# Moving the start-up loads of an attention-and-FFN kernel into one casting queue, with single-head transposes and masks by matmul

## The chip, the cores and the metric

The kernel runs on one core of a Trainium2 chip. The metric is device time in microseconds (us), the median over several executions; lower is better. A ratio between two kernels is the mean time of the one's fast runs over the mean of the other's fast runs of the same rounds, so it is not quite the ratio of the medians that stand beside it. An interval in brackets is a 95% interval. "Same" means within 2%.

Engine names in the profile: PE is TensorE's matmuls, PEld its weight loads, DVE VectorE, ACT ScalarE, POOL GpSimd, SP SyncE. A group or timeline line names the source line (L323), the engine, the operation, the tiles as output<-input, and the shapes.

## The reference, cut to what matters

```python
# q, k, v: (batch 4, heads 8, seq 768, dim 64); mem_k, mem_v: (4, 8, 8, 64)
chunk, left_ctx, right_ctx = (32, 16, 8)
for c in range(seq // chunk):                    # each chunk of 32 queries sees its 56 or fewer
    q_c   = q[:, :, c*32 : c*32+32]              # neighbouring keys and 8 memory keys
    k_full = concat([mem_k, k[:, :, l_start:r_end]], axis=2)
    v_full = concat([mem_v, v[:, :, l_start:r_end]], axis=2)
    a = exp(scale * q_c @ k_full.T - max);  a = a / (sum(a) + 1e-9)
    out[:, :, c*32 : c*32+32] = a @ v_full
x = out.transpose(0, 2, 1, 3).reshape(3072, 512)
result = (maximum(x @ w_gate, 0) * (x @ w_val)) @ w_out     # d_ff = 1536
```

## The kernel before: the parts that matter here

The 3072 tokens are eight blocks of 384. Each block has an attention part (scores, exponentials, values) and an FFN part: 12 gate/value units of eight matmuls each (4 for `g_ps`, 4 for `vl_ps`), then three output units. While the FFN of one block keeps TensorE busy, the attention of the next is slipped in. Only the first two blocks (the "start blocks") have nothing to hide behind: their k, q and v come in as f32 by plain DMA, ACT and POOL cast them, TensorE transposes a pair of heads at a time, and DVE and ACT copy the result out of PSUM.

```python
class StartBlock(Block):                                   # blocks 0 and 1
    def cast_k(self, h):
        self.by_pair(nc.scalar.copy, self.kc, self.kr, h)  # ACT: f32 -> bf16, pairs of heads
    ...
    def keys_turn(self, h):
        ps = self.k_ps = fps.tile([128, 2, KR, KW], BF16, tag="gv", name="k_ps")
        for i in range(2):
            for s in range(KR):
                nc.tensor.transpose(ps[:, i, s, 0:KP], self.kc[:, 2 * h + i, s], ids["b"][:KP, :KP])
    # keys_copy: DVE copies k_ps to kb;  queries_copy: ACT and DVE copy q_ps to qz

class LaterBlock(Block):                                   # blocks 2 to 7
    ...
    def cast_k(self):
        ...
        pin(nc.vector.tensor_copy(self.kn[:, :, 0:3], view[:, :, 0:3]))
        nc.vector.tensor_copy(self.kn[0:24, :, 3], view[0:24, :, 3])      # NOT pinned
```

`pin` keeps an instruction in program order. An instruction without it may be placed elsewhere on its engine when the program is built. The last line above: the small cast of block 2.

```python
def warm(n, cols=256): ...                 # matmuls on zeros, to keep TensorE's clock up
warm(12, 512)
...
start_attention(b0, attention(b0, order0),
                lambda i: warm((5, 0, 4, 8, 2, 2, 2, 2, 2)[i]), first_weights)
...                                        # weights by POOL's queue, b1's k, q, v by SP's
def second_loads():
    for f in b2.pieces(sp):                # block 2's loads are issued first,
        f()
    pool_after(2, b2.qf[0:KROWS, 0, 0:1])
    for c in range(0, NDC, 4):             # then w_out, in three pieces
        pool(w_out_sb[:, c:c + 4], ...)
```

The softmax here doesn't subtract the row's maximum and nothing guards it: scores larger than these inputs give would overflow.

Of the kernel before, what the change touches and what calls it, by code (L numbers as in the profile page):

```python
# [17 lines left out]
def kernel(  # L18
# [33 lines left out]
    KW = KP + 2  # L52
    MEMCOL = 400
# [25 lines left out]
    ex_t = [wpool.tile([128, 4, 128], F16, name=f"ex{i}") for i in range(4)]  # L79
# [71 lines left out]
    def build_sel(T):  # L151
        base, starts = block_starts(T, KR * KROWS)
        sel = wpool.tile([KP, KR, NJ, 128], F16, name=f"sel{T}")
        (nc.vector if T == 0 else nc.gpsimd).memset(sel.bitcast(F32), 0.0)
        odd, first = regular(T)
        rel = [s - base for s in starts]
        for sl, r0, steps in ((sel[:, :, first:first + 3], rel[first], [[QB, 3]]),
                              (sel[:, :, odd], rel[odd], [])):
            nc.gpsimd.affine_select(
                out=sl, in_=sl, pattern=[[-1, KR]] + steps + [[1, 128]], compare_op=ALU.not_equal,  # L160
                fill=1.0, base=r0 - NMEM, channel_multiplier=-KR)
        nc.gpsimd.memset(sel[:, :, :, 0:NMEM], 0.0)
        sl = sel[:, :, :, 0:NMEM]
        nc.gpsimd.affine_select(
            out=sl, in_=sl, pattern=[[-1, KR], [0, NJ], [1, NMEM]], compare_op=ALU.not_equal,
            fill=1.0, base=KR * KROWS, channel_multiplier=-KR)
        return sel
# [3 lines left out]
    def kind_of(qb):  # L171
        return "first" if qb == 0 else ("last" if qb == NQB - 1 else "int")

    class Block:


        def __init__(self, n):
# [5 lines left out]
            self.qf = vpool.tile([128, H, NT * D], F32, name="qf")  # L183
# [12 lines left out]
        def load_q(self, h0, nh, dma):  # L196
            dma(self.qf[:, h0:h0 + nh], self.rows(q, h0, nh, MB * self.T, 128, NT * D))

    class StartBlock(Block):


        def make(self):
            self.kr = kf_t[self.n][0:KP].rearrange("p t h d -> p (t h d)").rearrange("p (h r) -> p h r", h=H)
            self.vr = vf_t[self.n][0:KP].rearrange("p t h d -> p (t h d)").rearrange("p (h r) -> p h r", h=H)
            self.kc, self.qc = kn_t[self.n][0:KP], qn_t[self.n]
            self.vc = spool.tile([KP, H, KR * D], F16, name="vc")

        def load_kv(self, which, h0, nh, dma):
            t, dst = (k, self.kr) if which == "k" else (v, self.vr)
            dma(dst[0:KROWS, h0:h0 + nh], self.rows(t, h0, nh, self.kbase, KROWS, KR * D))  # L210

        def load_mem(self, dma):
            for m, dst in ((mem_k, self.kr), (mem_v, self.vr)):
                dma(dst[KROWS:KP], self.mem(m, 0, H, KR * D))

        def cast_k(self, h):
            self.by_pair(nc.scalar.copy, self.kc, self.kr, h)

        def cast_q(self, h):
            self.by_pair(nc.scalar.copy, self.qc, self.qf, h)  # L220

        def by_pair(self, op, dst, src, h):
            op(dst[:, 2 * h:2 * h + 2].rearrange("p a s (x d) -> p a s x d", x=2),
               src[:, 4 * h:4 * h + 4].rearrange("p (a x) (s d) -> p a s x d", x=2, d=D))

        def cast_v(self, h):
            pin(nc.gpsimd.tensor_copy(self.vc[:, 4 * h:4 * h + 4], self.vr[:, 4 * h:4 * h + 4]))

        def keys(self, h):
            self.keys_turn(h)  # L230
            self.keys_copy(h, 0)
            self.keys_copy(h, 1)

        def keys_turn(self, h):
            ps = self.k_ps = fps.tile([128, 2, KR, KW], BF16, tag="gv", name="k_ps")
            for i in range(2):
                for s in range(KR):
                    nc.tensor.transpose(ps[:, i, s, 0:KP], self.kc[:, 2 * h + i, s], ids["b"][:KP, :KP])

        def keys_copy(self, h, part):  # L240
            ps = self.k_ps

            def band(row, mids, n):
# [3 lines left out]
            rel = [(s - self.kbase) // KR for s in self.starts]  # L247
            odd, first = regular(self.T)
            m = NMEM // KR
            nc.vector.tensor_copy(  # L250
                kb[:, part, first:first + 3, m:],
                bass.AP(tensor=ps.tensor, offset=ps.offset + KR * KW * part + rel[first],
                        ap=[ps.ap[0], [QB // KR, 3], [1, BAND // KR], [KW, KR]]))
            if part == 0:
                return
            nc.vector.tensor_copy(kb[:, :, odd, m:], band(rel[odd], [], BAND // KR))
            nc.vector.tensor_copy(kb[:, :, :, 0:m], band(KROWS, [[0, NJ]], m))  # L257
# [5 lines left out]
        def queries_turn(self, h):  # L263
            ps = self.q_ps = fps.tile([128, 2, NT, 128], BF16, tag="gv", name="q_ps")
            for i in range(2):
                for s in range(NT):
                    nc.tensor.transpose(ps[:, i, s], self.qc[:, 2 * h + i, s], ids["b"])
# [16 lines left out]
    class LaterBlock(Block):  # L284


        def make(self):
            self.kf, self.vf = kf_t[self.n % 2], vf_t[self.n % 2]
            self.kn, self.qn = kn_t[self.n % 2], qn_t[self.n % 2]
            self.qT = spool.tile([128, HP, NT, 128], BF16, name="qT")  # L290
            self.kT = spool.tile([128, HP, 512], BF16, name="kT")

        def pieces(self, dma):
# [18 lines left out]
            return [k01, k12, lambda: self.load_q(0, H, dma)] + [v1(j) for j in range(NJ)]  # L312
# [44 lines left out]
    def quad_stages(blk, j, g, x_big):  # L357
        st = {}
        kind, on_pe = kind_of(NJ * blk.T + j), blk.n == 0
# [99 lines left out]
    def load_start(blk):  # L459
        for h0 in (0, 4):  # L460
            blk.load_kv("k", h0, 4, sp)
            blk.load_q(h0, 4, sp)
            blk.load_kv("v", h0, 4, sp)

# [4 lines left out]
    gate = wpool.tile([128, 4], F32, name="gate")  # L469
    here = wpool.tile([1, 4], F16, name="here")  # L470

    def pool_after(i, src):
        pin(nc.gpsimd.tensor_copy(gate[0:KROWS, i:i + 1], src))
# [4 lines left out]
    b0.load_mem(nc.scalar.dma_start)  # L478
    load_start(b0)
    ids["b"] = wpool.tile([128, 128], BF16, name="ident_b")  # L480
    make_identity(nc, ids["b"])
    ids["h"] = wpool.tile([128, 128], F16, name="ident_h")
    nc.vector.tensor_copy(ids["h"], ids["b"])


    nc.vector.memset(w_out_sb[:, 0, :], 0.0)  # L486

    def warm(n, cols=256):
        ps = fps.tile([128, 512], F32, tag="gv", name="warm_ps")
        for _ in range(n):  # L490
            pin(nc.tensor.matmul(ps[:, 0:cols], lhsT=w_out_sb[:, 0, 0:128], rhs=w_out_sb[:, 0, 0:cols],  # L491
                                 start=True, stop=True))

    warm(12, 512)
    ids["chunks"] = build_chunks()
    lows["first"] = build_low("low_first", NMEM - 16)
    lows["int"] = build_low("low_int", NMEM)
    sels[0] = build_sel(0)
    for t in qz_t[0:1]:
        nc.vector.memset(t[0:D, :, 1].bitcast(F32), 0.0)  # L500
        nc.vector.memset(t[D:128, :, 0].bitcast(F32), 0.0)
    for t in vb_t:
        nc.vector.memset(t[:, :, :, D:VW], 1.0)
    for t in ex_t:
        nc.vector.memset(t[:, :, QB:128], 0.0)

    order0 = [(j, g) for g in range(2) for j in range(NJ)]

    def in_text_order(first):

        last = {}
        for ins in nc.cur_bb.bb.instructions[first:]:
            if ins.engine in (mybir.EngineType.PE, mybir.EngineType.DVE, mybir.EngineType.Activation):
# [5 lines left out]
    def start_attention(blk, att, fill, at_k1=lambda: None):  # L519

        scores, out_of, turn = ([a[i] for a in att] for i in range(3))
        blk.cast_k(0)
        blk.keys(0)
        blk.cast_q(0)
        blk.queries_turn(0)
        fill(0)
        blk.queries_copy(0)
        blk.cast_v(0)
        scores[0]()
        scores[1]()  # L530
        blk.values(0, 0)
        scores[2]()
        at_k1()
        fill(1)
        blk.cast_k(1)
        blk.values(2, 0)
        scores[3]()
        out_of[0]()
        out_of[1]()
        blk.keys(1)  # L540
        fill(2)
        blk.cast_q(1)
        blk.queries_turn(1)
        out_of[2]()
        blk.queries_copy(1)
        out_of[3]()
        blk.cast_v(1)
        fill(3)
        scores[4]()
        scores[5]()  # L550
        blk.values(0, 1)
        scores[6]()
        blk.values(2, 1)
        scores[7]()
        out_of[4]()
        fill(4)
        out_of[5]()
        turn[4]()
        fill(5)
        out_of[6]()  # L560
        turn[5]()
        fill(6)
        out_of[7]()
        turn[6]()
        fill(7)
        turn[7]()
        fill(8)

    def first_weights():
        pool_after(0, b0.kr[0:KROWS, 4, 0:1])  # L570
        weights(0, 512)

    first = len(nc.cur_bb.bb.instructions)
    start_attention(b0, attention(b0, order0), lambda i: warm((5, 0, 4, 8, 2, 2, 2, 2, 2)[i]), first_weights)
    in_text_order(first)

    weights(512, 1024)
    weights(1024, 1536)
    sp_after(0, w_gate_sb[0:1, 0, 1024:1025])
    b1.load_mem(sp)  # L580
    load_start(b1)
    sels[1] = build_sel(1)
    for t in qz_t[1:]:
        nc.gpsimd.memset(t[0:D, :, 1].bitcast(F32), 0.0)
        nc.gpsimd.memset(t[D:128, :, 0].bitcast(F32), 0.0)
    for name, qb in (("first", 0), ("int", 1), ("last", NQB - 1)):
        masks[name] = build_mask("mask_" + name, qb)

    order = [(j, g) for j in range(NJ) for g in range(2)]
# [29 lines left out]
    first = len(nc.cur_bb.bb.instructions)  # L619
    for u in range(8):  # L620
        dff[0][u]()

    def second_loads():
# [64 lines left out]
```

## Time and profile before

| | before |
|---|---|
| device time, median of the first 3 runs | 254.0 us (252.83 to 254.27) |
| span of the profiled run | 251.2 us |
| TensorE busy | 233.0 us, 93% |
| block 0's first gate matmul | 25.37 us |
| block 1's first gate matmul | 57.20 us |

The page's first two parts, for the kernel before. In the slices each digit is the busy share in tenths of 1/40 of the span (6.3 us here); PEclk is the clock granted to TensorE in the same tenths.

```profile
PE 233.0 (93%) x1647; PEld 139.4 (55%) x1647; DVE 137.2 (55%) x358; ACT 116.7 (46%) x221; POOL 58.3 (23%) x116
PE   7689987779979998999999999999999999999993
PEclk9799999997999999999999999999999999999999
```

TensorE is nearly full from slice 13 on (nines, with one 8). Whatever a change of the start can bring lies in the first twelve digits.

The timeline of TensorE, kernel before. Columns: start in us, length in us, engine, line, operation, tiles, shapes, count; in brackets the idle time just before and what ended it.

```profile
7.75 0.57 PE L238 MATMUL k_ps<-ident_b,kn_103 114*128 114x114 bf16 x8 [1.55 <-ACT kn_103 L223]
25.37 0.81 PE L427 MATMUL g_ps<-xT,w_gate_sb 128*128 128x384 f16 x4 [0.34 <-ACT xT L401]
36.79 0.57 PE L238 MATMUL k_ps<-ident_b,kn_104 114*128 114x114 bf16 x8 [0.86 <-ACT kn_104 L223]
57.20 1.44 PE L427 MATMUL g_ps<-xT,w_gate_sb 128*128 128x384 f16 x4 [0.57 <-ACT xT L401]
```

Four marks: block 0's keys are turned at 7.75 us, its FFN starts at 25.37, block 1's keys are turned at 36.79 and its FFN starts at 57.20. From the last mark to the end of the span it takes 251.2 - 57.2 = 194.0 us, nearly all of it TensorE's own work. The first group of that FFN took 1.44 us for four matmuls where 0.81 is usual.

Two windows of the kernel before. Columns after the window and its length: busy us and instruction count of PE, PEld, DVE, ACT and POOL, then the granted clock, the DMA engines' busy share and GB/s.

```profile
36.00:46.00 10.00, 7.74 (x77) 5.79 (x78) 6.57 (x14) 6.54 (x12) 3.36 (x5) 1.00 1.10 207
46.00:58.00 12.00, 8.15 (x84) 5.41 (x83) 9.66 (x29) 6.62 (x13) 8.99 (x16) 0.95 1.19 227
```

And the small cast of block 2 on DVE, from the timeline of the kernel before:

```profile
44.71 0.85 DVE L319 CAST kn_103<-kf_99 24x512 bf16<-24x512 f32 x1 [0.56 <-DMA kf_99<-in_k_dram]
```

Being free, it was placed in the middle of block 1's attention. It waited for its data by 0.56 us there.

### The profile page before, as it was taken

The page shows a single profiled execution, that of the slowest core. Times are in us where ns is not written, and L with a number is a line of the kernel's source. Part 1 is how long each engine was busy: PE and PEld are TensorE (multiplying, and loading weights), DVE is VectorE, ACT ScalarE, POOL GpSimd, SP SyncE. Part 2 cuts the span into 40 slices and gives each one's busy share as a digit, 9 for nine tenths or more (in the row PEclk, how much of TensorE's full clock was granted, in tenths as well). Part 3 has the DMA queues.
Part 4 walks back from the last instruction along what each step waited for, and adds up shares of the span by engine and source line. Part 5 has one row for each costly group of instructions (what it writes and reads, how often), then busy time and mean ns, then how long its engine had stood idle before and what let it go on. Part 6 is the DMA issues. An engine that isn't in the chain of part 4 may idle for free.

```text
span 251.2 us, 4576 instructions
## 1 busy us (share of the span) xinstructions
PE 233.0 (93%) x1647; PEld 139.4 (55%) x1647; DVE 137.2 (55%) x358; ACT 116.7 (46%) x221; POOL 58.3 (23%) x116
## 2 busy tenths in 40 slices
PE   7689987779979998999999999999999999999993
PEld 2477545454546445664566456645665566556541
DVE  5375336882577306995289527952796178404410
ACT  1666355653544245672467146714672366223311
POOL 8789002682001203034004012340022000000000
PEclk9799999997999999999999999999999999999999
DMA  6999999998798678998599949994999401130012
GB/s 185 235 176 207 163 274 202 243 203 138 149 251 156 157 175 215 253 130 186 171 266 133 195 142 260 169 147 155 263 161 171 143 0 33 37 119 7 3 42 84
DMA packets 95873, 40.17 MB, mean 160 GB/s; under 512 B 76330, under 2 KB 92778, under 8 KB 95850
## 3 DMA queue, kind: packets, MB, share of 16 engines
q1 hardware_dynamic: 91062, 35.12, 66.5%
q0 software_dynamic: 4752, 4.72, 11.7%
q8 instruction: 13, 0.21, 0.4%
q14 instruction: 10, 0.08, 0.1%
q10 hardware_dynamic: 36, 0.03, 0.1%
HBM read 30.43 MB, written 6.29 MB: 146 GB/s over the span
## 4 chain that ended last, share of the span: by engine, by line
PE 72%; DMA 17%; DVE 4%; POOL 2%; issue 2%; SPq 1%; ACT 1%; DVEq 0%; POOLq 0%
PE out_ps L446 24%; PE vl_ps L431 21%; PE g_ps L427 21%; DMA kf_99<-in_k_dram 7%; DMA w_gate_sb<-in_moe_w_gate_dram 4%; PE s_ps L364 4%; DMA qf<-in_q_dram 3%; PE o_ps L382 2%; DMA qT<-qn_105 2%; DMA qT<-qn_106 1%; SPq L88 1%; DVE x_big L387 1%; PE v_ps L279 1%; POOL w_gate_sb L91 1%; POOL w_val_sb L91 1%
## 5 line engine op out<-in xcount | busy, mean ns | idle before, releaser
L436 DVE TENSOR_TENSOR gvT<-vl_ps,g_relu 128x384 f16<-128x384 f32 x96 | 53.2, 556 | 73.4 <-PE vl_ps L431 71.8
L427 PE MATMUL g_ps<-xT,w_gate_sb 128*128 128x384 f16 x384 | 79.0, 329 | 0.9 <-ACT xT L401 0.9
L431 PE MATMUL vl_ps<-xT,w_val_sb 128*128 128x384 f16 x384 | 79.1, 328 | 0.2 <-DVE kb L257 0.2
L434 ACT ACTIVATE g_relu<-g_ps 128x384 f16<-128x384 f32 x96 | 46.9, 491 | 41.5 <-PE g_ps L427 20.7
L446 PE MATMUL out_ps<-w_out_sb,gvT 128*128 128x512 f16 x288 | 63.6, 379 | 0.0
L431 PEld LDWEIGHTS <-w_val_sb 128*128 128x128 f16 x384 | 37.7, 98 | 25.4 <-issue 0.7
L427 PEld LDWEIGHTS <-w_gate_sb 128*128 128x128 f16 x384 | 36.3, 98 | 19.7 <-issue 2.0
L446 PEld LDWEIGHTS <-gvT 128*128 128x128 f16 x288 | 28.1, 98 | 32.6
L449 ACT COPY o_sb<-out_ps 128x512 f32<-128x512 f32 x24 | 14.1, 586 | 51.2 <-PE out_ps L446 47.9
L387 DVE TENSOR_TENSOR x_big<-o_ps,rinv 96x256 f16<-96x256 f32 x64 | 26.6, 418 | 1.6
L364 PEld LDWEIGHTS <-kb 128*128 128x128 bf16 x128 | 10.2, 98 | 8.0 <-issue 5.8
L364 PE MATMUL s_ps<-qz_97,kb 128*128 128x192 bf16 x64 | 11.3, 251 | 2.8 <-DVE qz_97 L353 1.9
L372 ACT ACTIVATE ex_110<-s_ps 128x384 f16<-128x384 f32 x16 | 7.9, 491 | 12.5 <-PE s_ps L364 9.8
L385 DVE RECIPROCAL rinv<-o_ps 96x4 f32<-96x4 f32 x64 | 10.7, 169 | 5.2 <-PE o_ps L382 5.1
L300 POOL COPY vf_101<-memv 8x512 f32<-8x512 f32 x12 | 7.8, 686 | 23.0 <-DMA memv<-in_mem_v_dram 23.0
L364 PE MATMUL s_ps<-qz_98,kb 128*128 128x192 bf16 x64 | 10.1, 244 | 3.0 <-DVE qz_98 L272 2.1
L372 ACT ACTIVATE ex_112<-s_ps 128x384 f16<-128x384 f32 x16 | 7.8, 491 | 7.4 <-PE s_ps L364 5.6
L491 PE MATMUL warm_ps<-w_out_sb 128*128 128x256 f16 (+1 forms) x39 | 9.5, 382 | 1.3 <-DVE w_out_sb L486 1.3
L372 ACT ACTIVATE ex_111<-s_ps 128x384 f16<-128x384 f32 x16 | 7.8, 490 | 4.3 <-PE s_ps L364 4.1
L372 ACT ACTIVATE ex_113<-s_ps 128x384 f16<-128x384 f32 x16 | 7.9, 493 | 4.1 <-PE s_ps L364 4.1
L336 POOL CAST vb_107<-vf_102 128x512 f16<-128x512 f32 x4 | 2.6, 650 | 25.6 <-DVE rinv L385 20.6
L336 POOL CAST vb_108<-vf_102 128x512 f16<-128x512 f32 x4 | 2.8, 709 | 21.2 <-PE s_ps L364 18.6
(135 smaller groups left out, 206.8 us busy)
## 6 DMA issues: line engine op xcount, KB each, us to landing
out_dram<-o_sb SPq DMA_DIRECT2D x24, 256.0 KB
qf<-in_q_dram SPq DMA_DIRECT2D x6, 768.0 KB
vf_101<-in_v_dram SPq DMA_DIRECT2D x12, 240.0 KB
vf_102<-in_v_dram SPq DMA_DIRECT2D x12, 240.0 KB
kf_99<-in_k_dram SPq DMA_DIRECT2D x9, 256.0 KB
kf_100<-in_k_dram SPq DMA_DIRECT2D x9, 256.0 KB
qf<-in_q_dram SPq DMA_DIRECT2D x4, 384.0 KB
w_gate_sb<-in_moe_w_gate_dram POOLq DMA_DIRECT2D x3, 512.0 KB, 7.8
```

What stands on the lines that cost most here:

```text
L300: pin(nc.gpsimd.tensor_copy(self.vf[0:NMEM, j], memv[self.b]))
L364: nc.tensor.matmul(s_ps[:, i], lhsT=blk.kb[:, 2 * g + i, j, :], rhs=blk.qz[:, 2 * g + i, :, :, 32 * j:32 * j + 32], start=True, stop=not o ...
L372: nc.scalar.activation(e, s_ps.rearrange("p a x s c -> p (a x) (s c)"), ACT.Exp, scale=SCALE)
L385: nc.vector.reciprocal(rinv, o_ps[0:QB, :, D:D + 1])
L387: nc.vector.tensor_tensor(out=x_big[:, 256 * g:256 * g + 256].rearrange("p (h d) -> p h d", h=4), in0=o_ps[0:QB, :, 0:D], in1=rinv_b, op=A ...
L427: nc.tensor.matmul(g_ps, lhsT=w_gate_sb[:, f, 128 * m:128 * m + 128], rhs=blk.xT[:, f, :], start=(f == 0), stop=(f == NFC - 1))
L431: nc.tensor.matmul(vl_ps, lhsT=w_val_sb[:, f, 128 * m:128 * m + 128], rhs=blk.xT[:, f, :], start=(f == 0), stop=(f == NFC - 1))
L434: nc.scalar.activation(g_relu, g_ps, ACT.Relu)
L436: nc.vector.tensor_tensor(out=state["gvT"][:, m].rearrange("p t j c -> p j t c"), in0=vl_ps.rearrange("p (j t c) -> p j t c", j=NJ, t=NT), ...
L446: nc.tensor.matmul(out_ps, lhsT=state["gvT"][:, m, t].rearrange("p j c -> p (j c)"), rhs=w_out_sb[:, m, :], start=(m == 0), stop=(m == NDC ...
L449: nc.scalar.copy(o_sb, out_ps)
L491: pin(nc.tensor.matmul(ps[:, 0:cols], lhsT=w_out_sb[:, 0, 0:128], rhs=w_out_sb[:, 0, 0:cols], start=True, stop=True))
```

## The change

The intent: ACT and POOL need not cast anything for the start blocks if the DMA queue does it on the way, as POOL's queue already does for the weights in the kernel before. So k, q and v of blocks 0 and 1, and all weights, go in one row through POOL's queue, in the order in which they are needed. The cast no longer puts heads into pairs, so each head is transposed alone, into its half of PSUM's partitions (16 and 12 transposes in place of 8 and 6). Block 1's masks are added by matmul as block 0's were. The sel matrices are copies of one shifted pattern. All instructions of the start, on four engines, are held in the order of the text. Block 2's loads are issued by SP once the first third of w_out is there. The warm-up matmuls are rearranged along the way.

The diff, cut to its core:

```diff
 class StartBlock(Block):
+    def load(self, which, h0, nh=4):
+        if which == "q":
+            pool(self.qc[:, h0:h0 + nh], self.rows(q, h0, nh, MB * self.T, 128, NT * D))
+        else:
+            t, dst = (k, self.kc) if which == "k" else (v, self.vc)
+            pool(dst[TOK0:KP, h0:h0 + nh], self.rows(t, h0, nh, self.kbase, KROWS, KR * D))
-    def cast_k(self, h): ...            # and cast_q, by_pair, cast_v
+    def turn(self, ps, src, h, n, rows):
+        for i in range(2):
+            for s in range(n):
+                for x in range(2):
+                    nc.tensor.transpose(ps[D * x:D * x + D, i, s, 0:rows],
+                                        src[:, 4 * h + 2 * i + x, D * s:D * s + D], ids["b"][:rows, :rows])
     def keys_copy(self, h):
-        nc.vector.tensor_copy(kb[:, :, odd, m:], ...)
-        nc.vector.tensor_copy(kb[:, :, :, 0:m], ...)
+        nc.scalar.copy(kb[:, :, odd, TOK0:], ...)
+        nc.scalar.copy(kb[:, :, :, 0:TOK0], ...)
...
-    kind, on_pe = kind_of(NJ * blk.T + j), blk.n == 0
+    kind, on_pe = kind_of(NJ * blk.T + j), blk.n < NSTART
...
-    warm(12, 512)
+    warm(16)                                     # 256 columns each
+    b0.cast_mem(nc.vector)                       # 2 x (2x2048) f32 casts on DVE
...
-    start_attention(b0, attention(b0, order0), lambda i: warm((5, 0, 4, 8, 2, 2, 2, 2, 2)[i]), first_weights)
+    start_attention(b0, attention(b0, order0), lambda i: (warm(2), rest_of_b0() if i == 1 else None))
     weights(512, 1024)
     weights(1024, 1536)
+    for h0 in (0, 4):
+        for which in "kqv":
+            b1.load(which, h0)
+    for c in range(0, NDC, 4):
+        pool(w_out_sb[:, c:c + 4], ...)
...
-    for u in range(8):
+    for u in range(9):
         dff[0][u]()
     start_attention(b1, ...)
-    second_loads()
+    in_text_order(text0)                         # PE, DVE, ACT and POOL, from the very start
+    sp_after(0, w_out_sb[0:1, 0, 0:1])           # SP waits for w_out's first third,
+    for f in b2.pieces(sp):                      # then loads block 2
+        f()
-    prepare(b2, (hooks, 1), (hooks, 2), (hooks, 3), (hooks, 5))
+    prepare(b2, (hooks, 5), (hooks, 6), (hooks, 7), (hooks, 8))
```

## The prediction

> **What bounds the kernel now.** From about 72 us on TensorE is full: the stretches from 100 to 225 us show PE busy 25.0 of every 25 us. The change does not touch this. What it can move is the start-up. The chain of waits and the timeline show it: first k by DMA until about 5.4 us, an ACT table load (1.28), ACT casts (1.04, 0.83), scores at 10.5, first gate matmul at 25.4, block 1's attention from 36.8, block 1's first gate matmul at 57.2 (its first groups at a cold clock, about 1.5 us lost), then 1.85 us of waiting for block 2's queries. The question is when block 1's gate matmuls start.
>
> **Removed.** ACT casts of k and q (1.04 + 0.83 us per half, four halves), Pool casts of v (4 x 1.04), DVE masks in block 1 (8 x about 0.42), Pool's sel builds (1.55 + 0.63 us each), the table load on the chain.
>
> **Added.** Transposes 8 to 16 and 6 to 12 per half: by 0.07 us each, 1.0 us more per half. 16 mask matmuls in block 1 (about 1.3 us). All start-up bytes pass one queue with a GpSimd issue each (the Trainium skill, "DMA: Bandwidth & Descriptors", SWDGE vs HWDGE vs iDMA: only GpSimd's queue casts). In the trace this queue landed one 1.05 MB (f32) weight piece per 2.55 us, about 410 GB/s of source.
>
> **Two new waits on DVE.** The skill ("TensorE: Matmul & The Clock Gate", table of specifications) calls VectorE's queue strict FIFO; the built order shows:
> 1. Between block 0's last x_big and its first gvT: sel copies, two 1536-element zero copies (about 1.0 us each, as the 128x1536 casts), two 2048-element casts (about 1.3 each): 5.5 to 6.5 us. PSUM lets TensorE run about 2.5 units ahead, so about 2 us show.
> 2. After the seventh gvT stands block 2's small k cast (24x512, 0.56 us of wait before). SP issues its data only after the first third of w_out landed. Before that the queue must carry about 12.5 MB of f32: at 340 to 410 GB/s, with its start and a hole of about 2 us, it lands at about 39 us (36 to 43), an estimate; five SP issues and 256-byte rows add about 6. DVE then stands from about 35 to 45 us; the eighth gvT and block 1's key copies wait behind it.
>
> **Sum (estimates).** Block 0's gate matmuls start at about 23 us instead of 25.4: 2.4 gained. DVE free at about 45; from there block 1's attention takes 16 to 19 us (before: 19.8 from key copy to gate): start at 61 to 64 instead of 57.2, 4 to 6 lost. Cold clock and the wait for block 2's queries shrink: about 3 gained. Net near zero. Without the wait on the small cast I would expect 245 to 248.
>
> **Prediction: 253 us, 246 to 259.5 (8 in 10).** Faster 0.25, within 2% 0.62, slower 0.13.
>
> **What would show it.** First gate matmul at 22 to 25 us. In DVE's waits: the 24x512 cast waiting 5 to 12 us for a DMA of k around 35 to 46 us, TensorE idle then. Block 1's first gate matmul at 58 to 65. From block 2 on nothing changes.
>
> **What would make it wrong.** The queue is faster than I think and the small cast waits little (faster, down to 244). Or block 1's attention is much shorter without casts and masks. Or GpSimd stalls: each issue waits for the eighth before it, and block 1's sel select stands behind the last w_out issue (slower, up to 262).

## The result

The changed kernel took 266.14 us (265.01 to 266.79, 4 runs) beside 253.53 us (252.83 to 254.27, 4 runs) for the kernel before: ratio 1.0492 [1.0441, 1.0543], slower by 5%. The predicted time was 253 us, and 266 lies outside the range given. Both profiled runs: spans of 263.3 and 251.2 us.

The page's first two parts, changed kernel:

```profile
PE 236.1 (90%) x1718; PEld 141.7 (54%) x1718; DVE 138.6 (53%) x357; ACT 114.4 (43%) x224; POOL 63.7 (24%) x120
PE   5788990398899699999999999999999999999994
PEclk9589996579999999999999999999999999999999
```

TensorE has a hole in the seventh and eighth slices (6.6 us each here), and the clock digit falls to 5 in the eighth: the hole is followed by slow matmuls. The groups of the page tell who stood there, and for whom. Columns: busy us and mean ns, then idle us before them and what ended it.

```profile
L431 PE MATMUL g_ps<-xT,w_gate_sb 128*128 128x384 f16 x384 | 79.5, 330 | 12.0 <-DVE gvT L440 11.3
L261 ACT COPY kb<-k_ps 128x240 bf16<-128x240 bf16 x4 | 1.4, 358 | 17.3 <-DVE kb L257 15.3
L323 DVE CAST kn_103<-kf_99 24x512 bf16<-24x512 f32 x3 | 1.3, 421 | 12.7 <-DMA kf_99<-in_k_dram 12.7
```

TensorE and ACT wait for DVE, and DVE for a DMA: the small cast of block 2, 0.5 us of work, waits 12.7 us. The timelines of TensorE and DVE, changed kernel, show the four marks, the stop and block 1's first scores (55.92):

```profile
6.94 0.59 PE L244 MATMUL k_ps<-ident_b,kn_103 114*64 114x114 bf16 x16 [2.36 <-POOL chunks L144]
26.44 0.81 PE L431 MATMUL g_ps<-xT,w_gate_sb 128*128 128x384 f16 x4 [0.35 <-ACT xT L405]
38.53 0.59 PE L244 MATMUL k_ps<-ident_b,kn_104 114*64 114x114 bf16 x16
50.39 1.44 PE L431 MATMUL g_ps<-xT,w_gate_sb 128*128 128x384 f16 x4 [11.26 <-DVE gvT L440]
55.92 0.25 PE L368 MATMUL s_ps<-qz_98,kb 128*128 128x192 bf16 x1
70.94 0.81 PE L431 MATMUL g_ps<-xT,w_gate_sb 128*128 128x384 f16 x4 [0.35 <-ACT xT L405]
...
36.11 0.56 DVE L440 TENSOR_TENSOR gvT<-vl_ps,g_relu 128x384 f16<-128x384 f32 x1 [0.74 <-PE vl_ps L435]
49.38 0.49 DVE L323 CAST kn_103<-kf_99 24x512 bf16<-24x512 f32 x1 [12.71 <-DMA kf_99<-in_k_dram]
```

The Trainium skill ("TensorE: Matmul & The Clock Gate", Architectural detail) calls VectorE's queue strict FIFO. This trace agrees: the next `gvT` product had both its inputs by about 38.6 us and ran at 49.80, right behind the cast.

The chain of waits, changed kernel (start, length, what), says why the data came so late:

```profile
16.78 13.77 DMA w_gate_sb<-in_moe_w_gate_dram
30.83 11.56 DMA w_out_sb<-in_moe_w_out_dram
42.41 0.73 SPq L89
44.84 4.35 DMA kf_99<-in_k_dram
49.80 0.55 DVE gvT L440
50.39 1.44 PE g_ps L431 x4
```

POOL's queue works off its bytes in order. w_out's first third lands at 42.41, behind everything the start needs, and only then does SP issue block 2's loads. The small cast's data are there at 49.3.

The windows of the changed kernel, beside those shown of before:

```profile
36.00:46.00 10.00, 3.13 (x33) 1.90 (x31) 0.56 (x1) 0.98 (x2) 5.64 (x28) 0.79 1.30 203
46.00:58.00 12.00, 7.36 (x47) 4.28 (x47) 3.98 (x8) 3.50 (x9) 3.68 (x6) 0.61 1.03 222
```

Sum by marks: block 1's FFN starts 70.94 - 57.20 = 13.7 us later, and the rest takes 263.3 - 70.9 = 192.4 us in place of 194.0. That is 13.7 - 1.6 = 12.1 us, the difference of the two spans.

Two things in these lines were not foreseen. Block 0's FFN starts at 26.44, later than before (25.37) although its keys are turned 0.8 us earlier; and after the hole the first groups of four matmuls take 1.44 us in place of 0.81 (the recorded clock is 0.61 on average over 46 to 58 us). The skill (same page, "Part 1: The HAM clock gate") says that TensorE falls back to half its clock after an idle window of about 3.4 us and needs about as long of work to return; the hole of 11.26 us and the 1.44 us after it agree. So long a hole is not needed, though: in the kernel before, the first group at 57.20 took the same 1.44 us, and no wait that its timeline lists in the 15 us before that was longer than 1.23 us.

### The profile page after: what moved, and what is told of

The parts are those of the page before. It is cut to its first block, busy times and chain, and to the rows that moved or that the text cites. A ratio compares the mean times of both kernels' runs of the same rounds, so it can differ in the third digit from the quotient of the medians.

```text
span 263.3 us, 4699 instructions
## 1 busy us (share of the span) xinstructions
PE 236.1 (90%) x1718; PEld 141.7 (54%) x1718; DVE 138.6 (53%) x357; ACT 114.4 (43%) x224; POOL 63.7 (24%) x120
## 4 chain that ended last, share of the span: by engine, by line
PE 75%; DMA 13%; POOL 5%; DVE 2%; issue 2%; ACT 1%; SPq 1%; POOLq 0%; DVEq 0%
PE out_ps L450 24%; PE g_ps L431 21%; PE vl_ps L435 21%; DMA w_gate_sb<-in_moe_w_gate_dram 5%; DMA w_out_sb<-in_moe_w_out_dram 4%; PE s_ps L368 4%; PE o_ps L386 3%; DMA kf_99<-in_k_dram 2%; DMA qT<-qn_105 2%; PE v_ps L282 1%; POOL w_gate_sb L92 1%; SPq L89 1%; POOL w_val_sb L92 1%; POOL qn_105 L92 1%; DVE qz_98 L357 1%
## 5 line engine op out<-in xcount | busy, mean ns | idle before, releaser
L368 PE MATMUL s_ps<-qz_97,kb 128*128 128x192 bf16 x64 | 11.5, 258 | 4.1 <-DVE qz_97 L357 2.0
L304 POOL COPY vf_101<-memv 8x512 f32<-8x512 f32 x12 | 7.8, 684 | 23.8 <-DMA memv<-in_mem_v_dram 23.8
L368 PEld LDWEIGHTS <-kb 128*128 128x128 bf16 x128 | 10.6, 100 | 5.0 <-issue 3.0
L368 PE MATMUL s_ps<-qz_98,kb 128*128 128x192 bf16 x64 | 10.8, 244 | 2.0 <-DVE qz_98 L275 0.9
L340 POOL CAST vb_107<-vf_102 128x512 f16<-128x512 f32 x4 | 3.0, 745 | 36.1 <-DMA vf_102<-in_v_dram 36.1
L498 PE MATMUL warm_ps<-idle 128*128 128x256 f16 x38 | 7.9, 337 | 1.2 <-DVE idle L478 1.2
L261 ACT COPY kb<-k_ps 128x240 bf16<-128x240 bf16 x4 | 1.4, 358 | 17.3 <-DVE kb L257 15.3
L323 DVE CAST kn_103<-kf_99 24x512 bf16<-24x512 f32 x3 | 1.3, 421 | 12.7 <-DMA kf_99<-in_k_dram 12.7
L340 POOL CAST vb_108<-vf_102 128x512 f16<-128x512 f32 x4 | 3.1, 772 | 19.4 <-DMA vf_102<-in_v_dram 19.4
L340 POOL CAST vb_109<-vf_102 128x512 f16<-128x512 f32 x4 | 3.0, 743 | 19.2 <-PE vl_ps L435 17.9
L304 POOL COPY vf_102<-memv 8x512 f32<-8x512 f32 x12 | 7.4, 653 | 0.0
```

The costliest lines, as they stand in the source:

```text
L304: pin(nc.gpsimd.tensor_copy(self.vf[0:NMEM, j], memv[self.b]))
L340: pin(nc.gpsimd.tensor_copy(self.vb[:, j, :, 0:D], self.vf[:, j]))
L368: nc.tensor.matmul(s_ps[:, i], lhsT=blk.kb[:, 2 * g + i, j, :], rhs=blk.qz[:, 2 * g + i, :, :, 32 * j:32 * j + 32], start=True, stop=not o ...
L498: nc.tensor.matmul(ps[:, 0:256], lhsT=idle[:, 0:128], rhs=idle, start=True, stop=True)
```

## The experiments

Theory A: the 12.7 us wait of the small cast, and nothing else, makes the change slower; it comes from the place of one instruction in DVE's queue together with the late issue of its data. Rivals: the backlog of DVE work ahead of block 0's first `gvT`, the longer chain of copies at the start (D), the casting queue with the hole in it (B). The first needs no run: in the changed kernel's trace TensorE lost at most 0.3 us to that backlog (point 4 of the explanation below).

Eleven kernels ran, all correct, in three groups; the kernel before ran in the same rounds with medians of 253.31, 253.30 and 253.27 us (the second group's eleven runs held one slow run and the third's two; their fast runs alone have 253.11 and 253.21).

| run | what it is | us, median of the fast runs | ratio to before |
|---|---|---|---|
| changed kernel | | 266.14 | 1.0492 [1.0441, 1.0543] |
| e1_pin | changed + cast pinned | 252.36 | 0.9954 [0.9909, 0.9999] |
| e2_tail | changed + its data issued early | 251.7 | 0.9951 [0.9910, 0.9992] |
| e3_chain | e1_pin + small key copies on DVE | 251.28 | 0.9927 [0.9883, 0.9971] |
| e4_issue | e1_pin + block 0's loads all issued first | 253.96 | 1.0025 [0.9984, 1.0066] |
| before_pin | kernel before + cast pinned | 254.10 | 1.0031 [0.9981, 1.0080] |
| h_pin_warm | e1_pin + longer warm-up | 251.00 | 0.9926 [0.9895, 0.9956] |
| f5_warm | e3_chain + longer warm-up | 250.36 | 0.9888 [0.9845, 0.9931] |
| f1_prep | e3_chain + block 2 prepared earlier | 250.84 | 0.9902 [0.9860, 0.9943] |
| f2_lock | e3_chain + casts off DVE | 252.15 | 0.9950 [0.9902, 0.9998] |
| g_best | all of the last three | 248.90 | 0.9835 [0.9791, 0.9879] |
| h_best2 | g_best + block 2's scores a unit later | 248.50 | 0.9822 [0.9792, 0.9851] |

### e1_pin and e2_tail: take the wait away, in two ways

The first holds the cast in the order of the text, where it comes after block 1's attention. The second leaves it free, but issues its two small loads ahead of SP's wait for w_out. Being free, it was then also placed elsewhere, as the trace below shows.

```diff
 # e1_pin
-            nc.vector.tensor_copy(self.kn[0:24, :, 3], view[0:24, :, 3])
+            tail = nc.vector.tensor_copy(self.kn[0:24, :, 3], view[0:24, :, 3])
+            if self.n == 2:
+                pin(tail)
 # e2_tail (the two loads are left out of b2.pieces)
+    sp(b2.kf[16:24, 3], b2.mem(mem_k, 0, H, D))
+    sp(b2.kf[0:16, 3], b2.rows(k, 0, H, b2.kbase + 384, 16, D))
     sp_after(0, w_out_sb[0:1, 0, 0:1])
```

> The changed kernel with one thing different: block 2's small k cast (24x512) is held in program order on the vector engine, so it stands behind block 1's gate products instead of before the eighth of block 0. Theory A (the changed kernel loses its time to that cast's 12.7 us wait for data that are issued late): the 11.3 us idle of the matrix engine at 39 us and the cold clock after it go, block 1's first gate matmul moves from 70.9 to 57-60 us, and the time falls from 266 to 251-254 us. Rival B (the loads come too late through the one casting queue, so the wait only moves to block 1's or block 2's own data): a wait of similar length shows up elsewhere and the time stays at 262 or more.

> The changed kernel with the cast left free to be placed, but its data (two loads, 48 KB) issued ahead of the load that waits for w_out. Theory A (it is the wait for data): the cast waits under 1 us wherever it stands, time 251-254 us as with the cast held back. Rival C (the place of the cast in the queue or the cast's own half microsecond matters, or the chain is bound elsewhere): 262 or more.

Measured: 252.36 us (251.22 to 253.15) and, over three fast runs, 251.7 us (251.63 to 252.40). A fourth run of e2_tail, the profiled one, took 353.47 us at a granted clock of 0.655: nothing is read from its durations, only the order of its instructions. Either edit takes some 14 us off the changed kernel. TensorE in e1_pin, the same marks, and block 1's next gate group and first scores:

```profile
6.81 0.97 PE L244 MATMUL k_ps<-ident_b,kn 114*64 114x114 bf16 x16 [2.05 <-POOL steps L155]
26.28 0.81 PE L433 MATMUL g_ps<-xT,w_gate_sb 128*128 128x384 f16 x4 [0.35 <-ACT xT L407]
38.37 0.59 PE L244 MATMUL k_ps<-ident_b,kn 114*64 114x114 bf16 x16
38.90 0.82 PE L433 MATMUL g_ps<-xT,w_gate_sb 128*128 128x384 f16 x4
42.30 0.24 PE L370 MATMUL s_ps<-qz,kb 128*128 128x192 bf16 x1
57.32 0.81 PE L433 MATMUL g_ps<-xT,w_gate_sb 128*128 128x384 f16 x4 [0.35 <-ACT xT L407]
```

Block 1's FFN starts at 57.32 in place of 70.94, and it runs at full clock. The cast itself ran at 66.73, among block 1's own products, and waited for nothing. SP's loads of block 2 start as late as in the changed kernel (w_out's third landed at 43.21), so it was never the loads that were late for TensorE: it was DVE that waited for them in the wrong place. Theory A holds. In e2_tail's trace the cast stands here on DVE:

```profile
17.73 0.39 DVE L325 CAST kn<-kf 24x512 bf16<-24x512 f32 x1
```

With its data issued early the cast was placed ahead of all of block 0's products, and again no wait is listed before it. So e2_tail is a second way to take the wait away, but no test of the data alone: its place changed too. Early data at the old place no run shows.

### before_pin: a control

The same pin in the kernel before. If pinning were a gain of itself, it would show here.

> A control: the kernel before, with the same cast of block 2 pinned in the order of the text. In its trace that cast waited 0.56 us at 44.7. If the pin in e1_pin worked only by taking away the 12.7 us wait, it does nothing here: ratio 0.998 to 1.002. If pinning that cast is a gain of itself (a better order on DVE), the ratio is 0.995 or lower.

Measured: 254.10 us, ratio 1.0031 [0.9981, 1.0080]: nothing. The cast now ran at 62.4 us in place of 44.7. Here, where the cast had waited 0.56 us, pinning gained nothing.

So the change without its accident is worth half a per cent (e1_pin 0.9954), where the prediction said "Without the wait on the small cast I would expect 245 to 248". The rest of the experiments ask where those 4 to 7 us went.

### e3_chain: the key copies on ACT

In the changed kernel ACT's two small copies of k_ps wait for DVE's two large ones, ACT's copy of q_ps comes after them, and DVE's copy of q_ps after that: one row of four. The edit puts the small copies back on DVE.

```diff
-            nc.scalar.copy(kb[:, :, odd, TOK0:], band(rel[odd], [], BAND // KR))
-            nc.scalar.copy(kb[:, :, :, 0:TOK0], band(0, [[0, NJ]], TOK0))
+            nc.vector.tensor_copy(kb[:, :, odd, TOK0:], band(rel[odd], [], BAND // KR))
+            nc.vector.tensor_copy(kb[:, :, :, 0:TOK0], band(0, [[0, NJ]], TOK0))
```

> As e1_pin, and the two small key copies (128x240, 128x64) back on the vector engine as in the kernel before. Theory D (the copies on the scalar engine wait for the vector engine's and then delay the query copies, a serial chain of about 0.6 us more in each of four halves): 1 to 3 us faster than e1_pin. Rival (the vector engine is the scarcer one in this stage): same as e1_pin or slower.

Measured: 251.28 us (250.51 to 252.12), ratio 0.9927, with an interval that overlaps e1_pin's. Its trace has the first gate matmul at 25.02 in place of 26.28, which looks like a gain of 1.3 us; but its keys were turned at 5.89 in place of 6.81, because the first load happened to land 0.9 us sooner in that execution (4.4 us after its issue, 5.3 in e1_pin, from the same instructions). From the keys' turn to the gate it is 19.13 against 19.47 us. So the trace alone would have oversold the edit. Even this stretch scatters: f1_prep below has e3_chain's start, instruction for instruction, and took 20.10 us. What does repeat is the second half, from the second turn of keys to the gate: 10.82 to 10.84 us in the four kernels with the small copies on ACT (changed kernel, e1_pin, e4_issue, h_pin_warm), 10.57 to 10.58 in the six with them on DVE (e3_chain, f5_warm, f1_prep, f2_lock, g_best, h_best2). That is 0.26 us from the row of copies; more is not shown.

### e4_issue: close the hole in POOL's queue

POOL's queue moves almost nothing at 6 to 7 and 9 to 11 us, because POOL builds masks between two issues. Here POOL issues all six loads of block 0 first.

```diff
     b0.load("v", 0)
+    b0.load("k", 4)
+    b0.load("q", 4)
+    b0.load("v", 4)
     steps = build_steps()
```

> As e1_pin, with all six loads of block 0 issued by the pool engine before it builds steps, chunks and masks, so that the casting queue has no hole between 6 and 12 us. Theory E (once the small cast no longer waits, the start is bound by the chain of engines and not by bytes): the first third of w_out lands 3 to 5 us earlier but the time is within 1% of e1_pin, perhaps 1 us slower because the masks come later. Rival B (the start is bound by the casting queue): 3 to 5 us faster than e1_pin.

Measured: 253.96 us, ratio 1.0025, 1.6 us slower than e1_pin. The loads come sooner (w_out's third by 41.56 us in place of 43.21, where 3 to 5 us were expected) and the masks later, and TensorE waits for the masks. Its timeline:

```profile
9.14 0.32 PE L370 MATMUL s_ps<-qz,kb 128*128 128x192 bf16 x1 [1.70 <-DVE qz L275]
11.45 0.34 PE L374 MATMUL s_ps<-chunks,low_first 128*128 128x192 bf16 x1 [1.99 <-POOL low_first L139]
```

So closing the hole in this way does not help. The edit moved loads and masks at once, so it does not show what the hole would cost by itself: rival B found no support, but it was not tested cleanly.

### f5_warm and h_pin_warm: the warm-up

In e3_chain's trace of TensorE the first scores of block 0 follow each other every 0.16 us, those of its second half every 0.08 us:

```profile
9.93 0.36 PE L370 MATMUL s_ps<-qz,kb 128*128 128x192 bf16 x1
10.09 0.36 PE L374 MATMUL s_ps<-chunks,low_first 128*128 128x192 bf16 x1
...
17.76 0.24 PE L374 MATMUL s_ps<-chunks,low_first 128*128 128x192 bf16 x1
17.84 0.24 PE L370 MATMUL s_ps<-qz,kb 128*128 128x192 bf16 x1
```

The skill ("TensorE: Matmul & The Clock Gate", Back-to-back issue gap) gives, for matmuls without the cost of their weight loads, N/1.2 ns between starts at half clock and N/2.4 + 2.5 ns at full clock; for N = 192 columns that is 160 and 82.5 ns, and the trace agrees to the digits it shows. So TensorE is at half clock until about 14 us. The change had cut the warm-up from 12 matmuls of 512 columns (to 6.2 us) to 16 of 256 (to 4.6 us), and those between keys and scores from 5 to 2 and 2 in the first half, from 4 and 8 to 2 and 2 in the second.

```diff
-    warm(16)
+    warm(30)
-    start_attention(b0, ..., lambda i: (warm(2), rest_of_b0() if i == 1 else None))
+    start_attention(b0, ..., lambda i: (warm(8 if i == 1 else 2), rest_of_b0() if i == 1 else None))
```

> The kernel of e3_chain, with 30 warm-up matmuls at the start in place of 16 and 8 in place of 2 ahead of block 0's first scores. Theory W: in e3_chain's trace block 0's first 16 score matmuls (10 to 12 us) follow each other every 0.16 us, the next 16 (17.7 to 19) every 0.08 us: TensorE runs at half rate until about 14 us because it stood from 4.6 to 5.9 us and again before the scores. Kept busy, the pitch is 0.08 us, and keys turn to first gate shortens from 19.1 us to 17.5 to 18.3; time falls by 0.8 to 1.6 us, ratio to before 0.986 to 0.990. Rival: from 6 to 14 us the chain is on DVE, ACT and the queue of loads and TensorE only waits less; keys turn to gate stays at 18.8 to 19.3 and the ratio at 0.992.

> The changed kernel with only two repairs: the small cast of block 2 pinned (as in e1_pin) and the longer warm-up (as in f5_warm); the two small key copies stay on ACT as the change has them. It tells apart what e3_chain and f5_warm mixed. If the warm-up alone is what counts: within 0.5 us of f5_warm's 250.4, ratio to before 0.987 to 0.991, keys turn to first gate about 17.5 us. If the key copies on ACT cost the 1 us that e3_chain seemed to gain: about 251.3, ratio 0.992 to 0.994, keys turn to first gate 18 to 18.5 us.

Measured: f5_warm 250.36 us (249.47 to 250.99), ratio 0.9888; h_pin_warm 251.00 us (250.29 to 251.57), ratio 0.9926. TensorE in f5_warm:

```profile
6.85 0.59 PE L244 MATMUL k_ps<-ident_b,kn 114*64 114x114 bf16 x16
9.78 0.24 PE L374 MATMUL s_ps<-chunks,low_first 128*128 128x192 bf16 x1
9.86 0.24 PE L370 MATMUL s_ps<-qz,kb 128*128 128x192 bf16 x1
24.32 0.81 PE L433 MATMUL g_ps<-xT,w_gate_sb 128*128 128x384 f16 x4 [0.35 <-ACT xT L407]
```

The pitch is 0.08 us from the first score on, and keys to gate takes 24.32 - 6.85 = 17.47 us; in h_pin_warm 17.95, in e1_pin 19.47. The other traces bear this out: the five with the short warm-up (e4_issue, with its late masks, left out) took 19.13 to 20.10 us and had the pitch of 0.16 us at their first scores, the four with the long one (g_best and h_best2 too) 17.05 to 17.95 and 0.08. So the warm-up takes at least 1.2 us off the start; from e1_pin to h_pin_warm, where it is the only difference, it is 1.5. The times agree in direction (252.36 to 251.00, 251.28 to 250.36), though the intervals of the ratios overlap. h_pin_warm's 251.00 lies between its two forecasts; its 0.6 us to f5_warm is within the intervals, and 0.26 of it is the second half's row of copies. The longer warm-up costs a little itself: in f5_warm k landed at about 6.3 us (4.9 after its issue at 1.38) and its turn stood behind warm-up matmuls until 6.85.

The kernel before took 17.62, and 16.64 in the trace of before_pin, whose start is the same. It too was at half clock in the first of these (a pitch of 0.16 us from 10.6 us, 0.08 from 12.98) and at full clock in the second (0.08 from 9.99). So its warm-up holds the clock in some executions only, and even with a warm TensorE the change makes this stretch no shorter than before.

### f1_prep: block 2's preparation

In e3_chain TensorE waits once more, for block 2's queries. Its data have landed by 59 us, and DMA is idle from there to 67: the preparation is hung too late.

```diff
-    prepare(b2, (hooks, 5), (hooks, 6), (hooks, 7), (hooks, 8))
+    prepare(b2, (hooks, 2), (hooks, 3), (hooks, 4), (hooks, 6))
```

> The kernel of the run e3_chain, with block 2's preparation (casts, turns, copies of its k and q) hung behind units 2, 3, 4 and 6 of block 1's FFN in place of 5, 6, 7 and 8. Theory P: after the start, the one place in e3_chain's trace where TensorE still stands is 70.1 to 73.3 us (0.67 us for a gvT, then 1.20 us for DVE qz L359); DMA is idle from 57 to 69 us and all of block 2's data has landed by 59, so the preparation is merely hung too late. Then TensorE is 10.0 of 10 us busy over 66 to 76 (it was 7.99) and the time falls by 1.5 to 2 us, ratio to before about 0.985. Rival: the transposes then collide with the fixed DVE queue of block 1's gvT, and the wait moves instead of going: ratio 0.99 to 0.995.

The wait before block 2's first scores, in the timelines of e3_chain, f1_prep and g_best, in this order:

```profile
73.31 0.49 PE L370 MATMUL s_ps<-qz,kb 128*128 128x192 bf16 x4 [1.20 <-DVE qz L359]
```

```profile
71.35 0.33 PE L370 MATMUL s_ps<-qz,kb 128*128 128x192 bf16 x2 [0.38 <-DVE qz L359]
```

```profile
69.00 0.33 PE L370 MATMUL s_ps<-qz,kb 128*128 128x192 bf16 x2 [1.16 <-DVE qz L359]
```

Measured: 250.84 us (249.97 to 251.13), ratio 0.9902. TensorE was busy 9.36 of 10 us over 66 to 76 (7.99 in e3_chain), and from block 1's gate to the end it took 249.1 - 57.8 = 191.3 us in place of 248.8 - 55.9 = 192.9: 1.6 us, as expected, though 10.0 busy of 10 was forecast. The median fell by only 0.4 us, and the ratio lies where the rival put it. In the profiled execution block 0's gate came at 26.99, 2.0 us later than in e3_chain, from the same instructions; how much of that scatter the other executions share no profile shows, so the gain in time stays less certain than the gain in the trace.

### f2_lock: DVE casts that hold POOL up

In the changed kernel POOL's identity took 1.21 + 1.15 us; in the kernel before 0.20 + 0.29. In between, DVE runs two f32 casts of 2x2048. The skill ("SBUF — State Buffer", "SBUF: two separate sides") says that DVE and GpSimd share one pair of ports, which certain DVE instructions take as an exclusive lock, for a whole instruction. The edit moves these casts to ACT and the zeroing of qz_97, which ACT did, to DVE.

```diff
-    clear_other_heads(nc.scalar.copy, qz_t[0])
+    b0.cast_mem(nc.scalar)
+    nc.vector.memset(qz_t[0][0:D, :, 1].bitcast(F32), 0.0)
+    nc.vector.memset(qz_t[0][D:128, :, 0].bitcast(F32), 0.0)
...
-    b0.cast_mem(nc.vector)
```

> The kernel of e3_chain, with the two 2x2048 f32 casts of block 0's memory rows moved from DVE to ACT and the zeroing of qz_97 moved from ACT to DVE. Theory L: at 2.9 to 5.3 us the DVE casts hold up Pool (ident_b's MEMSET took 1.21 us beside 0.20 before the change, its affine select 1.15 beside 0.29), so without them these two fall to about 0.2 and 0.3 us, block 0's v is issued 1.5 to 2 us earlier and the masks are done earlier; but the first keys turn waits for k's landing, so the first gate moves by 0 to 0.7 us and the time by 0 to 0.7 us (ratio 0.990 to 0.993). If instead the two Pool instructions are long in themselves, their durations stay at 1.2 and 1.15 us.

The timeline of DVE and POOL, changed kernel:

```profile
2.79 1.24 DVE L230 CAST kn_103<-kf_99 2x2048 bf16<-2x2048 f32 x1 [0.61 <-DMA kf_99<-in_mem_k_dram]
2.97 1.21 POOL masks.py:197 MEMSET ident_b<- 128x128 bf16 x1
3.96 1.29 DVE L230 CAST vc_122<-vf_101 2x2048 f16<-2x2048 f32 x1
4.25 1.15 POOL masks.py:199 TENSOR_SCALAR_AFFINE_SELECT ident_b<-ident_b 128x128 bf16<-128x128 bf16 x1
```

and f2_lock:

```profile
2.97 0.23 POOL masks.py:197 MEMSET ident_b<- 128x128 bf16 x1
3.28 0.29 POOL masks.py:199 TENSOR_SCALAR_AFFINE_SELECT ident_b<-ident_b 128x128 bf16<-128x128 bf16 x1
```

The two POOL instructions fell to 0.23 and 0.29 us, and block 0's v was issued at 3.52 in place of 5.40 (e3_chain). So DVE's casts did hold POOL up, and in the changed kernel each POOL instruction ended 0.15 us after a cast did (4.18 after 4.03, 5.40 after 5.25), as with a lock. But the time did not fall (252.15 us, ratio 0.9950, if anything above e3_chain's): POOL was 1.9 us sooner, and keys to gate took 19.93 us, within the scatter of e3_chain's start (19.13 and 20.10). The first keys still waited for their load, which in this execution landed 5.7 us after its issue.

### g_best and h_best2: the parts together

g_best is e3_chain with f1_prep's, f2_lock's and f5_warm's edits. h_best2 moves block 2's scores and copies a unit later, against the 1.16 us that g_best still waits (the third fence under f1_prep).

```diff
-    prepare(b2, (hooks, 2), (hooks, 3), (hooks, 4), (hooks, 6))
+    prepare(b2, (hooks, 2), (hooks, 3), (hooks, 4), (hooks, 7))
-        [(10, 11), (11, 12), (12, 13), (12, 13), (13, 14), (13, 14), (14, 15), (14, 15)])
+        [(11, 12), (12, 13), (12, 13), (13, 14), (13, 14), (14, 15), (14, 15), (15, 16)])
```

> All together: e3_chain, the earlier preparation of block 2, the DVE casts off Pool's way and the longer warm-up. If the gains add: 1.5 to 2 us for the preparation, 0.8 to 1.6 for the warm-up, 0 to 0.7 for the casts, below e3_chain's 251.3: 247 to 249 us, ratio to before 0.975 to 0.983. If nothing of it is critical but the preparation: about 249.5, ratio 0.985.

> The kernel of g_best with block 2's first scores one unit later (11 in place of 10), their successors packed, and the copies that prepare block 2 one unit later. In g_best's trace TensorE still stands 1.16 us at 67.8 to 69.0 before those scores, for DVE qz L359, whose data (the turned q) come by a DMA transpose. If that wait is all that is left: TensorE is 9.8 or more of 10 us busy over 66 to 76 (8.58 in g_best) and the time falls by 0.7 to 1.2 us to 247.7 to 248.2, ratio 0.979 to 0.981. Rival: the later attention then runs into the end of block 0's and 1's output units and block 2's FFN waits: 248.9 or more.

Measured: g_best 248.90 us (248.64 to 249.36), ratio 0.9835 [0.9791, 0.9879]; h_best2 248.50 us (247.69 to 248.83), ratio 0.9822 [0.9792, 0.9851]. Both beat the kernel before and the changed one. By the 2% rule their verdict against the kernel before is unclear: each interval reaches across 0.98. In h_best2 the wait before the scores is gone, and TensorE is busy 9.68 us over 66 to 76 (8.58 in g_best), but 22.27 over 76 to 100 (23.15): 1.10 gained, 0.88 given back right after. That wait moved more than it went, which is the rival's mechanism; the time lies between the two forecasts (247.7 to 248.2, and 248.9 or more).

## Why the prediction was wrong

It named the instruction and the wait, and undersized them. The step that failed is its sum for block 1's start: "DVE free at about 45", then "16 to 19 us", so "61 to 64". DVE was free at 49.8, the stretch after it took 21.1 us with a cold TensorE, and the start was at 70.94. Its gain at block 0, and so what it expected of the change without the wait, failed as well (point 3). Of its own signs, the cast waited 12.7 us (5 to 12), block 0's gate came at 26.44 (22 to 25) and block 1's at 70.94 (58 to 65); only the place of the wait was as said.

1. "DVE then stands from about 35 to 45 us." Right in kind, but the end was 4.4 us late. w_out's third landed at 42.4 (predicted 39, range 36 to 43), the cast's data 6.9 us later (predicted 6). DVE stood from 36.7 to 49.4 and was free at 49.8, 4.8 us later than reckoned. This is the largest single term.
2. "From there block 1's attention takes 16 to 19 us (...): start at 61 to 64". It took 70.94 - 49.80 = 21.1 us. The marks split it: 0.6 us to the next gate group, 5.53 from there to block 1's first scores (50.39 to 55.92), 15.02 from the scores to the gate. In e1_pin, undisturbed, the same two parts took 3.40 (38.90 to 42.30) and 15.02. So apart from the first 0.6 us, all that the stop added after its end, 2.1 us, lies where TensorE was cold: without waiting, it ran its first matmuls 0.32 us apart in place of 0.163. The prediction had the cold clock shrink, and it did at block 1's gate, but it came back after the stop. The rest is that the attention is no shorter for lack of casts and DVE masks. In e1_pin it takes 57.32 - 38.37 = 18.95 us from keys to gate with three FFN units inside; before, 20.41 with four. A unit is eight matmuls of 0.163 us, 1.30 us, so net of the units it is 15.0 against 15.2: hardly a gain. Which of the added transposes, mask matmuls and copies took the place of the removed work, no run shows.
3. "Block 0's gate matmuls start at about 23 us instead of 25.4: 2.4 gained." They started at 26.44, 1.1 lost: 3.4 us off. Keys were turned earlier (6.94 before 7.75), but keys to gate took 19.5 us in place of 17.6 (16.6 in before_pin). The longer warm-up takes 1.5 us off it, so a TensorE at half clock is part of it, and 0.26 is the row of key copies in the second half. As the kernel before was at half clock there too in its trace, how much of the loss against it is the smaller warm-up stays open. The diff showed the smaller warm-up, and the prediction did not read it.
4. "About 2 us show" of the DVE backlog. The first `gvT` came at 30.7, 5.2 us after the last `x_big` (5.5 to 6.5 reckoned), but the buffers in PSUM let TensorE run 3.5 units ahead, and it lost at most 0.3 us in 26 to 36 (9.59 busy against 9.93). Mis-sized, in the other direction.
5. "about 3 gained" later. It was 1.6 us.

The sum itself had a fault. Block 1's start at 61 to 64 was reckoned from DVE's wait, so block 0's earlier start could no longer be set against it; the middle of the prediction's own terms is 254.0 + (62.5 - 57.2) - 3 = 256.3 us, not 253. To that come 70.9 - 62.5 = 8.4 us at block 1's gate (4.8 of it from the later end of DVE's wait, 3.6 from the longer stretch after it) and 1.4 us of later gain that was not there: 266.1 us. That it meets the measured 266.14 so closely is in part luck: the marks come from one execution of each kernel, and these two took 252.85 and 265.01 us, 12.2 apart, where the medians lie 12.6 apart.

"Without the wait 245 to 248" failed for reasons 2 and 3: e1_pin's 252.4 is what was left, and the 248.5 of h_best2 took further repairs.

"From block 2 on nothing changes" held in the main: TensorE was busy 50.0 of 50 us over 150 to 200 in both kernels, and 49.45 (50.00 before) over 100 to 150.

## What to carry to other kernels

Before moving loads later or into one queue, list every instruction, on every strict-order engine, that waits for those loads, the small and the free-floating ones first: one unpinned 0.5 us cast cost 12.7 us of DVE and 14 us of the kernel, and pinning it or issuing its data early saved them. When an engine is relieved of casts, ask what the remaining row of copies and the clock of TensorE do to the same stretch: here block 1's attention, net of FFN units, went from 15.2 to 15.0 us. When two traces are compared in a start-up, measure from one event to the next and not from zero, and take more than one trace: the first load's landing moved by 1.0 us between executions of the same instructions (4.4 in e3_chain, 5.4 in f1_prep), and keys to gate by 1.0 us too.

## What the Trainium skill lacked or had wrong

- "DMA: Bandwidth & Descriptors", Anatomy of one DMA: the fit of 2.0 us plus bytes over 436 GB/s gives about 3.0 us for block 0's first load (448 KB of f32 read; an estimate from that page). From its issue on POOL to its landing the traces show 4.4 us (e3_chain) to 5.4 us (changed kernel, f1_prep) and 5.7 us (f2_lock); e3_chain and f1_prep issue it by the same instructions. The page gives no such scatter.
- "SBUF — State Buffer", SBUF: two separate sides: the blocking is seen here, and its size for plain POOL instructions, which the page doesn't give: a memset of 128x128 went from 0.23 to 1.21 us and an affine select from 0.29 to 1.15 us behind f32 casts of two partitions. In f1_prep, POOL's issue of a load took 1.43 us in place of 0.73 while such a cast ran, as the page's warning on descriptors says; but taking the casts away (f2_lock) did not make the first load land sooner.
- "TensorE: Matmul & The Clock Gate", Seeing it yourself (HAM trace caveats): the page warns that the recorded clock can be wrong. It was: in e3_chain the record shows 1.00 over 8 to 14 us, where the pitch of 0.16 us for 192 columns shows half clock; the changed kernel's record shows 0.50 there. Here the pitch of equal matmuls was the better reading.
- No page says that an unpinned instruction can be placed ahead of work that does not need it; here the 24x512 cast stood for 12.7 us ahead of the products that TensorE waited for.
